# Zero products at the start of PE, GpSimd's scalar steps behind its edge fixes, transposes released by another x tile

## The chip, the cores and the metric

The kernel runs on one core of a Trainium2 chip. A core has a matrix engine (PE), a vector engine (VectorE, DVE in the profile), ScalarE (ACT), GpSimd (POOL) and a queue engine that issues transfers (SyncE, SP). The metric is device time in microseconds (us); lower is better. The kernel before takes 342.55 us, the median of six runs that lie between 342.0 and 345.52.

## The reference, cut to what matters

Input x has 2048 rows of 1024 values. Two branches are computed from it and mixed by a gate, row by row:

```python
g = sigmoid((x * gate_w).sum(-1, keepdims=True))
a = irfft2(rfft2(x) * (w_r + 1j * w_i))            # branch A, over both axes
Lam_bar = exp(dt * Lam)                            # branch B: a state space model, 1024 states
B_bar   = ((Lam_bar - 1) / Lam)[:, None] * Bmat
h_t = Lam_bar * h_(t-1) + B_bar @ x_t              # for each row t
y   = 2 * real(h @ Cmat.T) + x * Dskip
out = g * a + (1 - g) * y
```

## The kernel before, in words

Branch A is a two-dimensional FFT done as matrix products. Branch B does the products with B first, rotates the result by tables of cosines and sines so that the complex recurrence becomes a real one, runs it as a scan on VectorE, rotates back and multiplies by C. The two branches are woven together: a small planner (`merge`-like loops at L770 to L776 over two generators with hand-given costs) decides in which order their steps are written, and below it a scheduler of the language orders the instructions of PE, VectorE and ScalarE. SP and GpSimd run in the order in which the program is written (L189).

**The opening, which the change touches.** x is loaded in eight tiles of 512 KB, `xts[0]` to `xts[7]` (`load_x`, L201): the first four into the pool buffers "h", the last four into the space that later holds C (CT0). In between SP issues G_sb, M(0) and W(0). The ScalarE queue loads ident, four short vectors (vec8) and the Fourier matrix FW.

**The fold stage** (`fstage`, L464) takes one x tile at a time. VectorE writes the sums and differences of its halves into a tile `eo` (L468 to L471: even sum, even difference, and the same for the mirrored half). The mirrored half has one column that has no partner; GpSimd fixes these edges with four ops of two elements per partition (L473 to L476). L473 is needed for the products with the sums, L475 and L476 for those with the differences. After each odd tile, PE multiplies the two tiles with FW: four PSUM tiles (`ps_f`) of eight products of 256 columns each (L495, L496), 128 products in the whole stage; three PSUM buffers are in turn. ScalarE casts each PSUM tile out with two copies (L499, L500), 32 in all. The `eo` tiles rotate through two buffers "u" (even tiles) and two buffers "cu" (odd tiles); vec8 and `angk`, the scratch of the angle reduction, take their turns in "cu" as well.

**The scalar chain** (`scalars`, L305) is a generator that is stepped once per x tile. From the vectors it derives, on 128 x 8 values: dt and r (Exp on ScalarE, L307, L314), angles and their sines (L308 to L312; the sine needs a load of another function table on ScalarE), a complex quotient (L317 to L328), its magnitude by a Newton root (L329 to L335, ending in rho), its angle by a half-angle formula and Arctan (L337 to L350), and beta. GpSimd does a few of these steps: nrho = -rho (L336), beta's first half (L351), and the pair sg (L353, L354). rho and nrho scale the PSUM copies of branch B (L411), beta and thp make the tables (`tables`, L366).

**The transposes.** Behind tile 3 (L716 to L728) a VectorE copy of one element into BT[0] (L717) makes the DMA transposes of B and x wait for an x tile: SP issues `load_BT(0)`, `load_xT(0)`, M(1), W(1), BT(1), M(2), FI, M(3), BT(2), BT(3) behind it. xT(0), 512 columns of the transposed x, is the moving operand of branch B's first products (L409).

After the fold stage, the FFT (`fd` L507, `bf_w` L527, `w_mul` L547, `bi` L559, `idm` L578, `fi` L598) and branch B (`ssm_pe` L403, `ssm_dve` L415) run woven together until about 160 us, then the products with C (`half`, L821) and the mix, until the end.

The function that is touched contains nearly everything. A block for zero products stands at L249 to L253 already, with a loop over `range(0)`: its fill is issued on GpSimd, its products are not.

Of the kernel before, what the change touches and what calls it, by code (L numbers as in the profile page):

```python
# [12 lines left out]
FP32 = mybir.dt.float32  # L13
# [9 lines left out]
P = 128  # L23
TC = 512
# [112 lines left out]
def kernel(  # L137
# [17 lines left out]
    nc = tc.nc  # L155
# [18 lines left out]
    BT = cpool.tile([P, 8, 2, 8, P], BF16, name="BT")  # L174
    tab = cpool.tile([P, 8, 3, TC], BF16, name="tab")
# [4 lines left out]
    rp = ctx.enter_context(tc.tile_pool(name="rp", bufs=2))  # L180
    sm = ctx.enter_context(tc.tile_pool(name="sm", bufs=2))
    psU = ctx.enter_context(tc.tile_pool(name="psU", bufs=2, space=PSUM))
# [13 lines left out]
        nc.scalar.dma_start(out=vec8[:, i, :], in_=src.rearrange("(j p) -> j p", p=P))  # L196
    nc.scalar.dma_start(out=FW_sb, in_=cFW)

    x_v = x.rearrange("(p b) d -> p b d", b=16)

    def load_x(jj):  # L201
        if jj < 4:
            xt = hp.tile([P, 2, D], BF16, name="xt", tag="h")
        else:
            xt = CT0[:, 2 * (jj - 4):2 * (jj - 4) + 2].rearrange("p a b d -> p a (b d)")
        nc.sync.dma_start(out=xt, in_=x_v[:, 2 * jj:2 * jj + 2, :])
        return xt

    def load_BT(jb):
        for ri, src in enumerate((B_B_re, B_B_im)):  # L210
            nc.sync.dma_start_transpose(out=BT[:, jb, ri], in_=src[P * jb:P * (jb + 1), :])

    def load_xT(c, halves=(0, 1)):
        for h in halves:
            r0 = TC * c + 256 * h
            nc.sync.dma_start_transpose(out=xT[:, :, r0:r0 + 256], in_=x[r0:r0 + 256, :])
# [13 lines left out]
    def load_M(g):  # L230
        m = fr.tile([P, 6, P], BF16, name="MM", bufs=4)
        nc.sync.dma_start(out=m, in_=cMM[g])
        MM[g] = m

    def load_W(g):
        w = Wtiles[g % 2]
        for ri, src in enumerate((A_w_r, A_w_i)):
            rows = bass.AP(src.tensor, src.offset + g * 513, [[32 * 513, 64], [((32 - 2 * g) if g else 16) * 513, 2], [1, 513]])
            (nc.sync if g < 2 else nc.gpsimd).dma_start(out=w[:, ri, 0:513], in_=rows)
        WT[g] = w  # L240

    xts = [load_x(jj) for jj in range(5)]
# [3 lines left out]
    xts.append(load_x(6))  # L246
    load_W(0)
    xts.append(load_x(7))
    warm = BT[:, 6, 0, 0:4, :].rearrange("p a c -> p (a c)")  # L249
    nc.gpsimd.memset(warm, 0.0)  # L250
    wps = psU.tile([P, TC], FP32, name="wps", tag="psu")
    for _ in range(0):
        nc.tensor.matmul(wps, lhsT=warm[:, 0:P], rhs=warm, start=True, stop=True)  # L253
    vps = psU.tile([P, 4, 8], BF16, name="vps", tag="psu")
    for i in range(4):
        nc.tensor.transpose(out=vps[:, i, :], in_=vec8[:, i, :], identity=ident[0:8, 0:8])
# [6 lines left out]
    def v8(name):  # L263
        if name in ("r_sb", "thp", "beta", "rho", "nrho"):
            return sp.tile([P, 8], FP32, name=name)
        scr_n[0] += 1
        return scr[:, scr_n[0] - 1, :]
# [9 lines left out]
    nc.vector.memset(chpi, HALF_PI)  # L277
    r_sb, beta, rho, nrho = (v8(n) for n in ("r_sb", "beta", "rho", "nrho"))
    ang = sp.tile([P, 16], FP32, name="ang")
    angk = rp.tile([P, 2, 16], FP32, name="angk", tag="cu")  # L280
    snc = sp.tile([P, 2, 16], FP32, name="snc")
    thp = ang[:, 0:8]
    sTC, cTC = snc[:, 0, 8:16], snc[:, 1, 8:16]
# [3 lines left out]
    def frac(xx, kk, ff):  # L287
        nc.vector.tensor_scalar(out=kk, in0=xx, scalar1=MAGIC, scalar2=-MAGIC, op0=ALU.add, op1=ALU.add)
        nc.vector.tensor_sub(out=ff, in0=xx, in1=kk)
        nc.vector.tensor_scalar(out=kk.bitcast(I32), in0=ff.bitcast(I32), scalar1=0x7FFFFFFF, scalar2=None,  # L290
                                op0=ALU.bitwise_and)

    def v16():
        scr_n[0] += 2
        return scr[:, scr_n[0] - 2:scr_n[0], :]

    def rsqrt(y, x, s):
        nc.vector.tensor_scalar(out=y.bitcast(I32), in0=x.bitcast(I32), scalar1=-0.5, scalar2=float(0x5F3759DF),
                                op0=ALU.mult, op1=ALU.add)
        for _ in range(2):  # L300
            nc.vector.tensor_mul(out=s, in0=y, in1=y)
            nc.vector.scalar_tensor_tensor(out=s, in0=s, scalar=-0.5, in1=x, op0=ALU.mult, op1=ALU.mult)
            nc.vector.scalar_tensor_tensor(out=y, in0=s, scalar=1.5, in1=y, op0=ALU.add, op1=ALU.mult)

    def scalars():  # L305
        dt, are = v8("dt"), v8("are")
        nc.scalar.activation(out=dt, in_=ldt, func=ACT.Exp)  # L307
        nc.vector.scalar_tensor_tensor(out=thp, in0=lim, scalar=INV2PI, in1=dt, op0=ALU.mult, op1=ALU.mult)  # L308
        nc.vector.tensor_scalar_mul(out=ang[:, 8:16], in0=thp, scalar1=float(TC))
        frac(ang, angk[:, 0, :], angk[:, 1, :])  # L310
        nc.scalar.activation(out=snc[:, 0, :], in_=angk[:, 1, :], func=ACT.Sin, scale=TWO_PI_LO)
        nc.scalar.activation(out=snc[:, 1, :], in_=angk[:, 0, :], func=ACT.Sin, scale=-TWO_PI_LO, bias=chpi)  # L312
        nc.vector.tensor_mul(out=are, in0=dt, in1=lre)
        nc.scalar.activation(out=r_sb, in_=are, func=ACT.Exp)  # L314
        yield
        dd, inv = v16(), v8("inv")
        nc.gpsimd.tensor_mul(out=dd, in0=lam, in1=lam)  # L317
        nc.gpsimd.tensor_add(out=dd[:, 0, :], in0=dd[:, 0, :], in1=dd[:, 1, :])
        nc.vector.reciprocal(out=inv, in_=dd[:, 0, :])
        yield  # L320
        nl, pr, c2 = v16(), v16(), v16()
        nc.vector.tensor_mul(out=nl, in0=snc[:, ::-1, 0:8], in1=r_sb.unsqueeze(1).to_broadcast([P, 2, 8]))
        nc.vector.tensor_scalar_add(out=nl[:, 0, :], in0=nl[:, 0, :], scalar1=-1.0)
        nc.vector.tensor_mul(out=pr, in0=nl, in1=lam)
        nc.vector.tensor_add(out=c2[:, 0, :], in0=pr[:, 0, :], in1=pr[:, 1, :])
        nc.vector.tensor_mul(out=pr, in0=nl[:, ::-1, :], in1=lam)
        nc.vector.tensor_sub(out=c2[:, 1, :], in0=pr[:, 0, :], in1=pr[:, 1, :])
        yield  # L328
        m2, rs, mag, s = v8("m2"), v8("rs"), v8("mag"), v8("s")  # L329
        nc.vector.tensor_mul(out=pr, in0=c2, in1=c2)  # L330
        nc.vector.scalar_tensor_tensor(out=m2, in0=pr[:, 0, :], scalar=1e-30, in1=pr[:, 1, :], op0=ALU.add, op1=ALU.add)
        rsqrt(rs, m2, s)
        nc.vector.tensor_mul(out=mag, in0=m2, in1=rs)
        yield
        nc.vector.scalar_tensor_tensor(out=rho, in0=mag, scalar=2.0, in1=inv, op0=ALU.mult, op1=ALU.mult)  # L335
        nc.gpsimd.tensor_scalar_mul(out=nrho, in0=rho, scalar1=-1.0)  # L336
        hd = v8("hd")  # L337
        nc.vector.tensor_add(out=hd, in0=mag, in1=c2[:, 0, :])
        nc.vector.tensor_scalar_max(out=hd, in0=hd, scalar1=1e-20)
        nc.vector.tensor_mul(out=m2, in0=hd, in1=mag)  # L340
        yield
        rsqrt(rs, m2, s)
        nc.vector.tensor_mul(out=m2, in0=m2, in1=rs)
        nc.vector.scalar_tensor_tensor(out=hd, in0=m2, scalar=float(np.sqrt(2.0)), in1=hd, op0=ALU.mult, op1=ALU.add)
        nc.vector.reciprocal(out=hd, in_=hd)
        yield
        nc.vector.tensor_mul(out=hd, in0=c2[:, 1, :], in1=hd)
        nc.vector.tensor_scalar(out=hd, in0=hd, scalar1=-1.0, scalar2=1.0, op0=ALU.max, op1=ALU.min)
        fq = v8("fq")
        nc.scalar.activation(out=fq, in_=hd, func=ACT.Arctan)  # L350
        nc.gpsimd.tensor_scalar_mul(out=beta, in0=thp, scalar1=-255.5)  # L351
        nc.vector.scalar_tensor_tensor(out=beta, in0=fq, scalar=-2.0 * INV2PI, in1=beta, op0=ALU.mult, op1=ALU.add)
        nc.gpsimd.tensor_scalar_mul(out=sg[:, :, 1], in0=sTC, scalar1=-1.0)  # L353
        nc.gpsimd.tensor_copy(out=sg[:, :, 0], in_=sTC)  # L354
        yield

    chain = scalars()
    for _ in range(1):
        next(chain, None)
# [353 lines left out]
    for jj in range(8):  # L713
        for _ in fstage(jj):
            pass
        if jj == 3:  # L716
            nc.vector.tensor_copy(out=BT[0:1, 0, 0, 0, 0:1], in_=xts[4][0:1, 0, 0:1])  # L717
            load_BT(0)
            load_xT(0)
            load_M(1)  # L720
            load_W(1)
            load_BT(1)
            load_M(2)
            nc.sync.dma_start(out=FI_sb, in_=cFI)
            if 4 == 4:
                load_M(3)
            load_BT(2)
            load_BT(3)  # L728
# [165 lines left out]
```

## Time and profile before

| What | us |
|---|---|
| Median of six runs | 342.55 |
| The profiled execution, its own time | 342.56 |
| Its span on the core | 340.8 |
| PE busy (share of the span) | 322.8 (95%) |
| DVE busy | 286.7 (84%) |
| ACT busy | 189.9 (56%) |
| POOL busy | 52.7 (15%) |
| First x tile in use (L468) | 5.26 |
| Last cast of the fold stage starts (L500) | 29.02 |
| First step on W in branch A (L551) | 35.08 |

Times in the profile count from the start of the span. A row of the timeline gives start, duration, engine, line, operation, output and inputs, how many were merged, and in brackets how long the engine had been idle and what ended it. Durations of neighbouring instructions overlap[...]: how fast a series runs is read from the distance between starts. A row of the waits gives who waited for whom, the total, the number of waits and the longest. PEclk is the clock that the throttle granted.

### The profile page before, as it was taken

Reading aid. Unit: us, or ns where it says so; the run is one execution under the profiler, and the core shown is the slowest. Engines: PE = TensorE matmul, PEld = TensorE weight load, DVE = VectorE, ACT = ScalarE, POOL = GpSimd, SP = SyncE. Lnnn points to the kernel's source line nnn. Section 1 sums busy time; section 2 is a strip of 40 time slices with the busy share of each in tenths; the row PEclk is TensorE's granted clock in tenths of the full one; section 3 lists DMA queues with packets and bytes.
Section 4 is the critical chain, followed back from the end, with each engine's and each line's share of the span. In section 5 each row is a group of like instructions: output and inputs, shape, how many; then the busy total and the mean of one; then the engine's idle time right before and its main releaser. Section 6 shows DMA issues by size and latency. Waiting matters only on the chain.

```text
span 340.8 us, 4928 instructions
## 1 busy us (share of the span) xinstructions
PE 322.8 (95%) x1804; PEld 172.8 (51%) x1804; DVE 286.7 (84%) x418; ACT 189.9 (56%) x266; POOL 52.7 (15%) x101
## 2 busy tenths in 40 slices
PE   2879999999999999998999999999999999999995
PEld 1666666665656566553444444444444444444442
DVE  2874899999999997999997999599999999982311
ACT  2789799889898777696253424441424424443200
POOL 4450322221211000000011002010120121201100
PEclk9999999999999999999999999999999999999999
DMA  6999999799879113022897063942855664969721
GB/s 241 388 219 196 170 234 219 143 241 165 197 176 180 63 62 125 31 92 94 250 220 211 0 185 67 266 90 71 188 111 135 156 170 108 242 191 245 201 65 46
DMA packets 70712, 54.97 MB, mean 161 GB/s; under 512 B 52768, under 2 KB 57888, under 8 KB 70688
## 3 DMA queue, kind: packets, MB, share of 16 engines
q1 hardware_dynamic: 64144, 38.75, 44.6%
q0 software_dynamic: 6192, 15.74, 21.7%
q8 instruction: 14, 0.23, 0.3%
q10 hardware_dynamic: 352, 0.17, 0.2%
q14 instruction: 10, 0.08, 0.1%
HBM read 21.61 MB, written 8.39 MB: 88 GB/s over the span
## 4 chain that ended last, share of the span: by engine, by line
PE 68%; DVE 12%; ACT 3%; DMA 3%; issue 2%; DVEq 0%; ACTq 0%; SPq 0%
PE psy L830 32%; PE psu L409 25%; PE ps_id L583 3%; DVE su L429 2%; DVE t L552 2%; DMA CT<-in_B_C_re_dram 2%; DVE Y L551 1%; DMA ya_scratch<-ya 1%; DVE Y L553 1%; PE ps_y L602 1%; DVE Y L554 1%; PE ps_d L512 1%; PE ps_y L605 1%; PE ps_y L603 1%; PE ps_y L604 1%
## 5 line engine op out<-in xcount | busy, mean ns | idle before, releaser
L409 PE MATMUL psu<-xT,BT 128*128 128x512 bf16 x512 | 120.0, 379 | 1.0 <-ACT u L411 1.0
L409 PEld LDWEIGHTS <-BT 128*128 128x128 bf16 x512 | 49.4, 98 | 56.2 <-issue 1.7
L429 DVE TENSOR_TENSOR_SCAN su<-r_sb,carry,cu 128x512 bf16<-128x512 f32 x48 | 57.8, 1265 | 0.4
L411 ACT ACTIVATE u<-psu,rho 128x512 bf16<-128x512 f32 x32 | 22.2, 694 | 51.7 <-PE psu L409 49.2
L411 ACT ACTIVATE u<-psu,nrho 128x512 bf16<-128x512 f32 x32 | 22.2, 693 | 37.6 <-PE psu L409 37.6
L830 PEld LDWEIGHTS <-h 128*128 128x128 bf16 x256 | 25.0, 98 | 30.2
L815 POOL DMA_DIRECT2D xf<-gac x16 | 16.3, 1019 | 117.6 <-DMA big<-in_B_C_im_dram 67.7
L837 DVE SCALAR_TENSOR_TENSOR o<-psy,om_f,xf 128x1024 bf16<-128x1024 f32 (+1 forms) x17 | 20.6, 1216 | 15.2 <-PE psy L830 15.2
L830 PE MATMUL psy<-CT,h 128*128 128x512 bf16 x128 | 28.9, 379 | 0.0
L830 PE MATMUL psy<-big,h 128*128 128x512 bf16 x128 | 28.9, 379 | 0.0
L812 ACT ACTIVATE gac<-gac,gf 128x1024 bf16<-128x1024 bf16 x16 | 18.2, 1139 | 18.5 <-DMA gac<-ya_scratch 18.5
L808 DVE TENSOR_TENSOR xc<-xc,dsk_bc 128x1024 bf16<-128x1024 bf16 x16 | 10.9, 684 | 15.4 <-DMA xc<-in_A_x_dram 14.9
L420 DVE TENSOR_TENSOR cu<-u,tab 128x2048 bf16<-128x2048 bf16 x16 | 19.5, 1218 | 1.9 <-ACT u L411 1.7
L830 PEld LDWEIGHTS <-xT 128*128 128x128 bf16 x128 | 12.5, 98 | 15.1
L830 PEld LDWEIGHTS <-big 128*128 128x128 bf16 x128 | 12.5, 98 | 15.1
L424 DVE TENSOR_TENSOR cu<-cu,su 128x2048 bf16<-128x2048 bf16 x16 | 19.6, 1228 | 0.4
L422 DVE TENSOR_TENSOR su<-u,tab 128x2048 bf16<-128x2048 bf16 x16 | 19.5, 1217 | 0.0
L512 PE MATMUL ps_d<-G_sb,big 128*128 128x256 bf16 (+3 forms) x128 | 18.6, 286 | 0.3 <-ACT X L539 0.3
L429 DVE TENSOR_TENSOR_SCAN su<-r_sb,cu 128x512 bf16<-128x512 f32 x16 | 18.7, 1208 | 0.1
L814 ACT ACTIVATE xf<-xc,om_f 128x1024 f32<-128x1024 bf16 x16 | 18.2, 1138 | 0.2
L496 PE MATMUL ps_f<-BT,eo 128*128 128x256 bf16 x64 | 16.5, 301 | 1.9 <-POOL eo L473 1.9
L495 PE MATMUL ps_f<-BT,eo 128*128 128x256 bf16 x64 | 16.5, 302 | 1.5 <-DVE eo L468 1.5
(163 smaller groups left out, 562.3 us busy)
## 6 DMA issues: line engine op xcount, KB each, us to landing
xf<-gac POOLq DMA_DIRECT2D x16, 512.0 KB, 6.8
ya_scratch<-ya SPq DMA_DIRECT2D x16, 256.0 KB, 2.0
xc<-in_A_x_dram SPq DMA_DIRECT2D x16, 256.0 KB, 4.4
gac<-ya_scratch SPq DMA_DIRECT2D x16, 256.0 KB, 3.7
out_dram<-o SPq DMA_DIRECT2D x15, 256.0 KB, 2.3
MM<-c_MM SPq DMA_DIRECT2D x16, 192.0 KB, 3.8
xt<-in_A_x_dram SPq DMA_DIRECT2D x4, 512.0 KB, 4.8
CT<-in_A_x_dram SPq DMA_DIRECT2D x4, 512.0 KB, 8.0
```

The source lines that it names most:

```text
L409: nc.tensor.matmul(psu, lhsT=BT[:, jb, ri, dblk, :], rhs=xT[:, dblk, TC * c:TC * (c + 1)], start=(dblk == 0), stop=(dblk == 7))
L411: nc.scalar.activation(out=u[:, jj, ri, :], in_=psu, func=ACT.Copy, scale=(nrho if ri else rho)[:, jb:jb + 1])
L420: nc.vector.tensor_mul(out=cu, in0=u, in1=tq[:, :, 0:1, :].to_broadcast(full))
L422: nc.vector.tensor_mul(out=su, in0=u[:, :, ::-1, :], in1=tq[:, :, 1:3, :])
L424: nc.vector.tensor_add(out=cu, in0=cu, in1=su)
L429: nc.vector.tensor_tensor_scan(out=su[:, jj, ri, :], data0=r_sb[:, jb:jb + 1].to_broadcast([P, TC]), data1=cu[:, jj, ri, :], initial=(0.0 ...
L495: nc.tensor.matmul(ps[:, jl], lhsT=lo, rhs=FW_sb[:, 0:2 * P], start=(i == 0), stop=False)
L512: nc.tensor.matmul(ps[:, lo:lo + w], lhsT=FX[:, q, 8 * g:8 * g + 8, :], rhs=G_sb[:, o:o + w], start=start, stop=stop, skip_group_check=True)
L812: nc.scalar.activation(out=gac, in_=gac, func=ACT.Copy, scale=gf[:, tb:tb + 1])
L814: nc.scalar.activation(out=xf, in_=xc, func=ACT.Copy, scale=om_f[:, tb:tb + 1])
L830: nc.tensor.matmul(psy[:, ds], lhsT=hs[c, jb // 2][:, jb % 2, ri, P * tq:P * (tq + 1)], rhs=CT[dh][:, jb, ri, :], start=(i == 0), stop=(i ...
L837: nc.vector.scalar_tensor_tensor(out=o[:, ds], in0=psy[:, ds], scalar=om_f[:, tb:tb + 1], in1=xfs[tb][:, ds], op0=ALU.mult, op1=ALU.add)
```

## The change

Four edits, all in the opening:

- The zero block moves to the front of PE's work, its fill goes to VectorE, and twelve products of 128 x 512 zeros into a PSUM tile that nobody reads are issued ahead of the vec transposes.
- `angk` moves from a pool buffer "cu" into a corner of the table space `tab`, which is written much later.
- nrho, beta's first half and sg are issued one step of the scalar chain later, in one group behind the edge fixes of tile 6, where nrho stood ahead of those of tile 4 and the others ahead of those of tile 6.
- The one-element copy that releases the transposes reads `xts[3]` instead of `xts[4]`.

```diff
+    warm = BT[:, 6, 0, 0:4, :].rearrange("p a c -> p (a c)")
+    nc.vector.memset(warm, 0.0)
+    wps = psU.tile([P, TC], FP32, name="wps", tag="psu")
+    for _ in range(12):
+        nc.tensor.matmul(wps, lhsT=warm[:, 0:P], rhs=warm, start=True, stop=True)
+
     x_v = x.rearrange("(p b) d -> p b d", b=16)
...
-    warm = BT[:, 6, 0, 0:4, :].rearrange("p a c -> p (a c)")
-    nc.gpsimd.memset(warm, 0.0)
-    wps = psU.tile([P, TC], FP32, name="wps", tag="psu")
-    for _ in range(0):
-        nc.tensor.matmul(wps, lhsT=warm[:, 0:P], rhs=warm, start=True, stop=True)
     vps = psU.tile([P, 4, 8], BF16, name="vps", tag="psu")
...
-    angk = rp.tile([P, 2, 16], FP32, name="angk", tag="cu")
+    angk = tab[:, 7, 2, 0:64].bitcast(FP32).rearrange("p (a n) -> p a n", a=2)
...
-        nc.gpsimd.tensor_scalar_mul(out=nrho, in0=rho, scalar1=-1.0)
         hd = v8("hd")
...
         nc.scalar.activation(out=fq, in_=hd, func=ACT.Arctan)
+        yield
+        nc.gpsimd.tensor_scalar_mul(out=nrho, in0=rho, scalar1=-1.0)
         nc.gpsimd.tensor_scalar_mul(out=beta, in0=thp, scalar1=-255.5)
...
         if jj == 3:
-            nc.vector.tensor_copy(out=BT[0:1, 0, 0, 0, 0:1], in_=xts[4][0:1, 0, 0:1])
+            nc.vector.tensor_copy(out=BT[0:1, 0, 0, 0, 0:1], in_=xts[3][0:1, 0, 0:1])
             load_BT(0)
```

## The prediction

> **What bounds it now.** I read the busy time in stretches first, to see which engine is full where, then the waits of the first 40 us, then the timeline of the first 37 us engine by engine. The chain of work that ended last is of no use here: it can be followed back only to 37.18 us, and the change lies before that. Columns of the first fence: stretch, its length, busy us of PE, PEld, DVE, ACT, POOL, then the clock shown, DMA share and GB/s.
>
> ```profile
> 5.00:10.00 5.00, 2.05 (x10) 1.11 (x11) 3.32 (x15) 1.73 (x4) 2.04 (x8) 1.00 0.97 340
> 10.00:15.00 5.00, 5.00 (x28) 3.65 (x29) 3.90 (x18) 3.37 (x8) 3.66 (x10) 1.00 1.01 397
> 20.00:25.00 5.00, 4.38 (x39) 3.70 (x40) 3.40 (x18) 3.39 (x9) 4.21 (x19) 1.00 1.22 227
> 25.00:30.00 5.00, 5.00 (x42) 3.59 (x40) 3.71 (x9) 5.00 (x11) 0.03 (x1) 1.00 0.76 161
> 80.00:120.00 40.00, 38.57 (x258) 24.27 (x256) 39.24 (x62) 34.61 (x49) 6.36 (x9) 1.00 0.74 150
> ```
>
> From 40 to 120 us VectorE is full (39.24 of 40), after 160 us the chain is back-to-back PE work. Neither has slack, so an earlier start of that stage passes through to the end. In the opening nothing is full throughout; ScalarE becomes full from 21.77 to 37 us. Its 32 PSUM casts (L499/L500) pace the fold stage:
>
> ```profile
> 8.14 1.28 ACT L311 ACT_TABLE_LOAD   x1
> ...
> 10.39 0.31 ACT L312 ACTIVATE snc<-angk,chpi 128x16 f32<-128x16 f32 x1 [0.20 <-DVE angk L290]
> 11.84 0.58 ACT L499 CAST big<-ps_f 128x512 bf16<-128x512 f32 x1 [1.14 <-PE ps_f L496]
> ...
> 19.46 0.70 ACT L500 CAST big<-ps_f 128x512 bf16<-128x512 f32 x1
> 21.77 0.58 ACT L499 CAST big<-ps_f 128x512 bf16<-128x512 f32 x1 [1.61 <-PE ps_f L496]
> 22.25 0.59 ACT L500 CAST big<-ps_f 128x512 bf16<-128x512 f32 x1
> ...
> 24.63 0.27 ACT L350 ACTIVATE scr<-scr 128x8 f32<-128x8 f32 x1
> 24.74 0.64 ACT L499 CAST big<-ps_f 128x512 bf16<-128x512 f32 x1
> ...
> 29.02 0.77 ACT L500 CAST big<-ps_f 128x512 bf16<-128x512 f32 x1
> ```
>
> The casts follow each other every 0.477 us (start to start; the durations overlap). The last starts at 29.02. The mark for this prediction is that start: all ScalarE work up to 37.3 us hangs on it without a gap. Lost in front of it: 1.61 us at 21.77, and a first cast only at 11.84. Why, the PE and POOL rows and the waits say:
>
> ```profile
> 13.94 0.42 PE L495 MATMUL ps_f<-BT,eo 128*128 128x256 bf16 x1
> 14.15 0.32 PE L496 MATMUL ps_f<-BT,eo 128*128 128x256 bf16 x1
> 14.30 0.27 PE L495 MATMUL ps_f<-BT,eo 128*128 128x256 bf16 x1
> 14.41 0.27 PE L496 MATMUL ps_f<-BT,eo 128*128 128x256 bf16 x1
> ```
> ```profile
> POOL nrho L336 <- DVE scr L338: 4.8, 1, 4.8
> PE ps_f L496 <- POOL eo L473: 1.9, 2, 1.4
> DVE eo L468 <- PE ps_f L496: 1.1, 1, 1.1
> ```
>
> Products start every 0.2145 us from 9.91 until 14.15, then every 0.109: PE runs at half rate until 4.24 us into its first unbroken stretch, although the clock column says 1.00 throughout; the cadence is what to read. And GpSimd stands at nrho (L336) until VectorE has rho (19.16), with the edge fix of x tile 4 (L473, run at 19.65) queued behind it; PE, then ScalarE, wait for that edge.
>
> **The change, part by part.** Spacings I use, all from the timeline: fold op to the next instruction 0.34; small op to an independent fold op 0.08 to 0.10; dependent small op to the next 0.20; product 0.109 (half rate 0.2145); cast 0.477. The built program's order of the new kernel gives the sequence on each engine.
>
> *Zero products.* The zero fill moves from GpSimd (0.52 at 0.84) to VectorE, which waits for x until 5.26: free. Twelve 128x512 products start near 1.2 us. The row for that shape at full rate is L409's 0.216 spacing (8 in 1.73); at half rate twice that, 0.43. Twelve take at most 5.2 us, to 6.4. Queued behind them are the four vec transposes, which wait for their loads until 6.58 anyway: cost 0 (if the cover were gone, one for one). What they buy: by this trace's 4.24 us the rate doubles near 5.5, before x arrives. The Trainium skill ("TensorE: Matmul & The Clock Gate", Part 1) says the gate opens after a busy window of about 3.4 us that runs freely, so about 4.6 to 5.6; it says also, against this change, that an idle window of that length closes it, and (Part 4) that transposes do not count as busy in the same way. Between 6.4 and 8.5 PE has only the four transposes and half a dozen products. The nearest row is kind: PE idles 1.37 us before 20.10 and comes back at 0.109. By the row the rate holds, by the strict reading it can fall. I take the row, and keep the other as a case.
>
> *angk leaves the "cu" buffers.* Not in the title, but the program order shows that it matters. Today x tile 1's sums take the buffer of the vec loads, so VectorE does tile 2 before it finishes tile 1: tile 1's L470 runs only at 10.27. Now tile 1 has a fresh buffer. It landed by 7.41 (SP's M load, which reuses its completion semaphore, issues then). So VectorE: L272 at 7.28, tile 1's L468 at 7.40, L470 at 8.07 to 8.49. PE has ten products from there to the end of the first tile needed: 10 x 0.109 + 0.2, so the first cast is at 9.8 instead of 11.84.
>
> *What is late next: ScalarE's order.* Two of those two microseconds are not kept. The table load (1.28 us), hidden in an idle stretch today, now stands behind cast 2: casts 1 and 2 with L314 between them from 9.8 to 10.95, table load to 12.25, L311 and L312 to 12.73, cast 3 at 12.65, where it was 12.79. And VectorE's L322 waits for L312: 12.75 instead of 11.74 (it has finished tile 3 and the release copy by 12.2, so it idles 0.5).
>
> *nrho, beta and sg behind the edge fixes.* Four GpSimd ops of 0.2 to 0.44 move, none is added. L473 of tile 4 no longer waits for rho: it can run once the tile has landed (11.6) and PE has freed its buffer (about 12). The PE stalls of 1.37 and 0.52 and ScalarE's 1.61 go. Queued behind the moved ops now are tile 7's edges and the wait for beta: four ops after tile 6's edges (about 20) end near 21.2, and tile 7's first fold op is at 21.2, Arctan at 22.2, so nothing waits. First user of nrho is the copy at 34.79: hidden.
>
> *What is late after that: the Arctan.* In the new order it stands behind cast 21 (today behind 22) and waits for VectorE's L348. From L322 to L348 there are 14 fold spacings x 0.34 (4.76), 10 x 0.08 (0.80), 16 x 0.20 (3.20), and five short ones (0.48): 9.24 us. L348 starts at 21.99, ends 22.2. ScalarE would reach cast 22 at 12.65 + 19 x 0.477 = 21.7, so it stands about half a microsecond. Arctan 22.25, cast 22 at 22.36, cast 32 at 22.36 + 10 x 0.477 = **27.13, 1.89 us before 29.02**. Without the Arctan wait it would be 26.6, 2.4 earlier; that is the upper bound.
>
> *Transposes released by the fourth tile.* In the built program the first transpose still waits for the completion semaphore that the fifth tile's load used (11.6; the profile of before has SPq L211 waiting 0.9 us for just that), and the copy now stands behind tile 3's four fold ops: 12.2. So SP is released 0.36 us later, not earlier, with every load behind it. The DMA engines are full with x, G, M and W until 17 us (350 to 418 GB/s), so between 0 and 0.4 us of that reaches the transposes; I take 0.4. xT's second half was issued at 20.02 and took 6.5 us: landed at 26.5, now up to 26.9. PE asks for it about 26.6. PE can stand until 27.1 before ScalarE's L524 is late. So it is hidden, by 0.2 us.
>
> Sum: the profiled execution has span 340.8 and time 342.56, 1.76 us around the span; the median of six runs is 342.55, the same. 342.56 - 1.89 = **340.7 us**.
>
> **Rivals.**
> *The clock falls back, or never rises.* Ten products at 0.2145 make the first cast 1.05 later, and it passes through table load, L322 and Arctan. Gain 0.84: 341.7. For: two thin microseconds; against: the row at 20.10.
> *The gain is given back later.* A transfer or another VectorE order in 40 to 160 us absorbs it: 342.5. For: the new order differs in a few places beyond 28 us (two L409 products earlier, L386 and L576 swapped). Against: VectorE is full there and the transfers are issued by the same stages, so they move too.
> *More than I think.* VectorE's small ops hide better between folds, the Arctan wait is gone: 340.1.
> *Slower: the transposes.* If later release lets all four first transposes issue as slowly as the second did (3.80 us each, 15.2 instead of 11.0 for the four), xT lands near 31.1. Each microsecond past 27.1 costs one, and past 29.0 the kernel is slower than before: 2.1 us, 344.7. For: the release is later in program order; against: the slow issues belong to the full DMA stretch that ends at 17.
> Were the third edit to do what it says, nothing would change: xT is not waited for.
>
> **Numbers.** Likeliest, 340.7 (own range 340.1 to 341.3): 0.60. More: 0.07. Clock: 0.15. Given back: 0.12. Slower: 0.06. About 0.5%, 1.71 us, can be told from no change, so faster is below 340.84: three quarters or more of the likeliest case and the "more" case, 0.54. Same 0.40, slower 0.06. Range 339.9 to 342.2: it leaves out the slow case, most of "given back" near 342.5, and a little below.
>
> **What would show it.** Right: product spacing 0.109 from tile 1 on; first cast near 9.8; table load between casts 2 and 3; no PE wait for L473; Arctan preceded by a short ScalarE wait on VectorE; last cast near 27.1; first transposes issued no earlier than 11.8. Wrong: products at 0.21 after 8.5; a ScalarE or PE wait for xT between 26 and 32; or a last cast at 27 with a first Y (L551, 35.08) not 1.9 earlier, or a span that does not follow it.

## The result, and the profile after

| | before | changed |
|---|---|---|
| Median, us (runs) | 342.31 (73) | 340.43 (36) |
| Ratio of the times, 95% interval | | 0.9941 (0.9926 to 0.9956) |
| The profiled execution, us | 342.56 | 339.83 |
| Its span, us | 340.8 | 337.8 |
| Last cast of the fold stage starts | 29.02 | 26.57 |
| First step on W (Y, L551, now L553) | 35.08 | 32.58 |
| First pm (VectorE's sums in branch A's last stage, L676, now L678) | 111.06 | 109.27 |

By the interval the gain is 1.5 to 2.5 us. Ratios, here and below, are of fast runs alone (a few runs, over 1.5% above the fastest, are left out), so they are not quite the quotient of the medians. In the changed file the lines lie one to two further on (L499 is L501, L551 is L553, L717 is L719), and in the moved zero block more.

The stretches of the changed kernel, columns as before:

```profile
5.00:10.00 5.00, 4.54 (x29) 2.61 (x28) 4.26 (x18) 1.25 (x4) 3.65 (x12) 1.00 0.99 336
20.00:25.00 5.00, 4.37 (x37) 3.26 (x36) 4.76 (x17) 4.41 (x11) 1.68 (x7) 1.00 1.26 192
80.00:120.00 40.00, 38.57 (x256) 24.25 (x255) 39.25 (x61) 34.62 (x48) 5.16 (x7) 1.00 0.67 147
```

PE's 2.05 us between 5 and 10 have become 4.54, of which about 1.5 are zero products; between 20 and 25 ScalarE's 3.39 have become 4.41. The stretch from 80 to 120 us is what it was (39.24 and 39.25 on VectorE), so nothing was won or lost there. ScalarE's timeline shows the casts:

```profile
8.96 0.58 ACT L501 CAST big<-ps_f 128x512 bf16<-128x512 f32 x1 [1.44 <-PE ps_f L498]
...
10.15 1.28 ACT L312 ACT_TABLE_LOAD   x1
...
11.76 0.56 ACT L501 CAST big<-ps_f 128x512 bf16<-128x512 f32 x1
...
21.70 0.21 ACT L350 ACTIVATE scr<-scr 128x8 f32<-128x8 f32 x1 [0.59 <-DVE scr L348]
21.82 0.57 ACT L502 CAST big<-ps_f 128x512 bf16<-128x512 f32 x1
...
26.57 0.70 ACT L502 CAST big<-ps_f 128x512 bf16<-128x512 f32 x1
```

The order is the one foretold: two casts, the table load behind them, an unbroken row of casts, one wait of 0.59 for VectorE at the Arctan, and the row again to the end. In this pair of executions the last cast comes 2.45 us earlier. Products on PE, and the GpSimd instructions that had stood in each other's way:

```profile
1.17 5.30 PE L203 MATMUL wps<-BT 128*128 128x512 bf16 x12 [1.17 <-DVE chpi L278]
...
7.28 0.27 PE L498 MATMUL ps_f<-BT,eo 128*128 128x256 bf16 x1
7.39 0.27 PE L497 MATMUL ps_f<-BT,eo 128*128 128x256 bf16 x1
...
8.42 0.28 PE L498 MATMUL ps_f<-BT,eo 128*128 128x256 bf16 x1 [0.41 <-DVE eo L472]
```
```profile
12.21 0.20 POOL L475 TENSOR_TENSOR eo<-CT 128x2 bf16<-128x2 bf16 x1
...
19.74 0.23 POOL L352 TENSOR_SCALAR nrho<-rho 128x8 f32<-128x8 f32 x1
```

The first separate products are 0.109 apart, so PE is at full rate from the first x tile on. The edge of tile 4 is fixed at 12.21 instead of 19.65, nrho follows at 19.74.

Not all of the 2.45 arrives. VectorE's timeline and ScalarE's, near 40 and 155 us:

```profile
39.06 0.69 DVE L553 TENSOR_TENSOR Y<-X,W 128x1028 bf16<-128x1028 bf16 x1 [0.44 <-ACT X L541]
40.48 0.69 DVE L554 TENSOR_TENSOR t<-X,W 128x1028 bf16<-128x1028 bf16 x1 [0.73 <-DMA W<-in_A_w_i_dram]
```
```profile
154.78 0.59 ACT L609 CAST ya<-ps_y 128x512 bf16<-128x512 f32 x1 [1.14 <-DMA ya_scratch<-ya]
```

The third step on W now waits 0.44 for ScalarE's copy of X and then 0.73 for its own W tile, neither of which it waited for before, and the first pm is only 1.79 earlier. The row of ScalarE had this form before:

```profile
158.65 0.59 ACT L607 CAST ya<-ps_y 128x512 bf16<-128x512 f32 x1 [3.22 <-DMA ya_scratch<-ya]
```

In this one execution of before, ScalarE waited 3.22 us for a store, and the span from the first pm to the end is 229.7 us instead of 228.5. That is why the two profiled spans differ by 3.0, though the opening accounts for 1.79 only: 2.45 - 0.66 given back near 40 us + 1.2 at the store = 3.0. The wait for the store goes with the zero products: it is 1.13 or 1.14 us in all nine profiled executions that have them, and 1.5 to 3.2 in the five that don't (the column "store" below). How the two hang together no run here shows, and so it is not shown either how much of the median's 1.88 us comes from the opening and how much from the store.

### The profile page after: what moved, and what is told of

Same layout as the page of the kernel before. It is cut to its first block, busy times and chain, and to the rows that moved or that the text cites. A ratio compares the mean times of both kernels' runs of the same rounds, so it can differ in the third digit from the quotient of the medians.

```text
span 337.8 us, 4956 instructions
## 1 busy us (share of the span) xinstructions
PE 326.1 (97%) x1816; PEld 173.0 (51%) x1816; DVE 287.5 (85%) x419; ACT 189.8 (56%) x266; POOL 52.0 (15%) x100
## 4 chain that ended last, share of the span: by engine, by line
PE 70%; DVE 16%; ACT 6%; DMA 5%; issue 2%; POOL 0%; DVEq 0%; ACTq 0%; POOLq 0%
PE psy L832 33%; PE psu L411 27%; PE ps_id L585 3%; DMA xt<-in_A_x_dram 3%; DVE t L554 2%; DVE su L431 2%; DMA W<-in_A_w_i_dram 2%; DVE Y L553 1%; DVE Y L555 1%; PE ps_y L604 1%; PE ps_y L607 1%; PE ps_y L606 1%; PE ps_y L605 1%; DVE Y L556 1%; ACT big L502 1%
## 5 line engine op out<-in xcount | busy, mean ns | idle before, releaser
L814 ACT ACTIVATE gac<-gac,gf 128x1024 bf16<-128x1024 bf16 x16 | 18.2, 1139 | 16.3 <-DMA gac<-ya_scratch 16.3
L816 ACT ACTIVATE xf<-xc,om_f 128x1024 f32<-128x1024 bf16 x16 | 18.2, 1139 | 0.2
L578 ACT CAST big<-ps_q 128x1024 bf16<-128x1024 f32 x16 | 16.3, 1020 | 2.9 <-PE ps_q L577 2.5
L526 ACT CAST X<-ps_d 128x1024 bf16<-128x1024 f32 x16 | 16.3, 1034 | 2.2 <-PE ps_d L514 1.8
```

Of the source, the lines that this page charges most:

```text
L526: nc.scalar.copy(out=X1, in_=ps)
L814: nc.scalar.activation(out=gac, in_=gac, func=ACT.Copy, scale=gf[:, tb:tb + 1])
L816: nc.scalar.activation(out=xf, in_=xc, func=ACT.Copy, scale=om_f[:, tb:tb + 1])
```

## The experiments

Before had medians of 342.27 (35 runs), 342.54 (19) and 342.54 (29) in the three groups (e1 to e4, e5 to e8, e9 to e12), and every ratio is to before. The first table has the times, the second where they come from, read from each kernel's profiled execution.

| | Kernel | Median (runs) | Ratio, 95% interval |
|---|---|---|---|
| e1 | before + zero products | 341.18 (12) | 0.9975 (0.9950 to 1.0000) |
| e2 | before + angk moved | 340.79 (12) | 0.9969 (0.9937 to 1.0001) |
| e3 | before + GpSimd steps moved | 341.49 (12) | 0.9986 (0.9958 to 1.0014) |
| e4 | changed, no zero products | 341.42 (12) | 0.9973 (0.9947 to 1.0000) |
| e5 | changed, again | 340.13 (7) | 0.9912 (0.9881 to 0.9944) |
| e6 | changed, angk back | 340.18 (8) | 0.9929 (0.9900 to 0.9959) |
| e7 | changed, GpSimd steps back | 339.97 (9) | 0.9935 (0.9903 to 0.9968) |
| e8 | changed + W(2) early | 339.66 (8) | 0.9909 (0.9879 to 0.9939) |
| e9 | changed, release back | 340.44 (12) | 0.9943 (0.9924 to 0.9962) |
| e10 | e4 once more | 341.05 (12) | 0.9958 (0.9932 to 0.9984) |
| e11 | changed, release later | 340.58 (12) | 0.9962 (0.9938 to 0.9987) |
| e12 | changed + early release + W(2) early | 339.43 (6) | 0.9921 (0.9891 to 0.9951) |

By their intervals none of e1, e2 and e3 is clear of no change, and the intervals of e4 to e12 all overlap that of the changed kernel: the times alone rank none of them.

The vectors' loads land at slightly different times in each execution. The column "from first use" counts from the row that first uses them (L270 of before at 7.18, L271 of the changed kernel at 7.09). Each row is one execution. The two of the changed kernel differ by 0.23 in this column, and an x tile that lands late adds up to a microsecond (e9), so a smaller difference between two rows proves little by itself. "Store" is ScalarE's wait for `ya_scratch` near 155 us.

| | Last cast | from first use | PE waits for xT | L554 waits for W(2) | first pm - last cast | store | span - first pm |
|---|---|---|---|---|---|---|---|
| before | 29.02 | 21.84 | - | - | 82.04 | 3.22 | 229.7 |
| changed | 26.57 | 19.48 | - | 0.73 | 82.70 | 1.14 | 228.5 |
| e1 | 28.05 | 21.34 | - | - | 82.01 | 1.14 | 228.5 |
| e2 | 26.38 | 19.92 | - | 0.61 | 82.71 | 2.83 | 229.3 |
| e3 | 27.74 | 21.14 | - | - | 82.26 | 1.56 + 0.25 | 228.5 |
| e4 | 25.95 | 19.51 | 1.86 | - | 83.91 | 3.03 | 229.5 |
| e5 | 26.47 | 19.25 | 1.03 | - | 83.23 | 1.14 | 228.5 |
| e6 | 26.68 | 19.52 | 0.44 | 1.02 | 83.24 | 1.14 | 228.6 |
| e7 | 27.93 | 21.08 | - | - | 82.01 | 1.13 | 228.6 |
| e8 | 27.02 | 19.60 | - | - | 82.27 | 1.13 | 228.5 |
| e9 | 27.64 | 20.77 | - | - | 82.25 | 1.13 | 228.5 |
| e10 | 27.04 | 19.52 | 0.84 | - | 82.89 | 1.50 + 0.31 | 228.6 |
| e11 | 26.96 | 19.71 | - | 0.71 | 82.69 | 1.14 | 228.6 |
| e12 | 27.73 | 20.80 | - | - | 82.25 | 1.14 | 228.5 |

Without a wait for xT or W(2), the first pm comes 82.01 to 82.04 us after the last cast where GpSimd's steps stand as before (before, e1, e7), and 82.25 to 82.27 where they are moved (e3, e8, e9, e12): there the third step on W waits 0.44 to 0.46 for ScalarE's copy of X. So the moved steps give back a quarter of a microsecond. A wait for xT or W(2) adds most of its length to that: 0.73 gives 82.70, 0.84 gives 82.89, 1.86 gives 83.91. And the span ends 228.5 us after the first pm, or up to 1.2 later with the longest waits at the store (before, e2, e4).

**e1, the zero products alone.** The edit puts the zero block of the changed kernel into before:

```diff
+    nc.vector.memset(warm, 0.0)
...
+    for _ in range(12):
+        nc.tensor.matmul(wps, lhsT=warm[:, 0:P], rhs=warm, start=True, stop=True)
```


> The kernel before with the zero products alone (twelve, fill on VectorE). Theory (the time follows the start of the fold stage's last cast, and the zero products pay because PE takes tile 1 at full rate): products 0.109 apart from the start; first cast near 10.3 instead of 11.84; the wait of PE for L473 of tile 4 stays, because nrho still stands ahead of it, so cast 17 comes with rho, near 20.9; last cast near 28.1, time about 0.9 us under before (341.4 where before is 342.3). Rival (the clock is the whole gain): last cast near 26.6 and 2.0 us under before. Rival (GpSimd's order is the whole gain): last cast at 29.0, no change.

Measured: 341.18. The first cast is at 11.39, which from the first use is where it was (4.68, before 4.66), and the two stalls in the middle stay: PE waits 1.7 us for L474 and ScalarE 1.41 at cast 17. From the first use, the last cast comes 0.5 earlier. But this execution is no test of full rate: PE's products are 0.2145 apart again from 10.56 to 13.93, and here the clock column (before the DMA share) shows it:

```profile
11.00:13.00 2.00, 2.00 (x11) 1.40 (x10) 1.95 (x11) 1.61 (x4) 1.84 (x6) 0.50 0.99 358
```

What the zero products alone would bring to the fold stage at the full clock is therefore not shown.

**e2, angk alone.**

```diff
-    angk = rp.tile([P, 2, 16], FP32, name="angk", tag="cu")
+    angk = tab[:, 7, 2, 0:64].bitcast(FP32).rearrange("p (a n) -> p a n", a=2)
```


> The kernel before with angk in the table space alone. In its program order tile 1 is done in one go, the table load stands behind cast 2, PE is at half rate, nrho still stands ahead of the edges. Theory: first cast near 9.6 to 10.9, but cast 3 and VectorE's L322 not before 13, rho about a microsecond later than 19.0, and the edges of tile 4 wait for it: last cast at 29 to 30, time 0 to 1 us over before. Rival (angk's place is the hidden key of the change): last cast at 28 or earlier, 1 us under before.

Measured: 340.79, and in the marks nearly the whole change: first cast at 8.65, last cast at 26.38, 19.92 from the first use. I had expected far less of it. GpSimd's timeline has the reason:

```profile
16.59 0.46 POOL L336 TENSOR_SCALAR nrho<-rho 128x8 f32<-128x8 f32 x1 [4.72 <-DVE scr L338]
17.01 0.20 POOL L473 TENSOR_TENSOR eo<-CT 128x2 bf16<-128x2 bf16 x1
```

nrho still stands ahead of tile 4's edge, but it ran at 16.59 where it had waited until VectorE had rho at 19.16. In the new order of VectorE, rho comes 4.8 us after L322 instead of 7.3; of these 2.5 us, 1.1 are VectorE's wait for PE's products in before (`DVE eo L468 <- PE ps_f L496`), which is gone. The edge is fixed at 17.01, and what was a PE stall of 1.37 and 0.52 is 0.54 and 0.25. So angk's place weakens the GpSimd stall too, which the prediction ascribed to another edit.

**e3, the GpSimd steps alone.**

```diff
-        nc.gpsimd.tensor_scalar_mul(out=nrho, in0=rho, scalar1=-1.0)
...
+        yield
+        nc.gpsimd.tensor_scalar_mul(out=nrho, in0=rho, scalar1=-1.0)
```


> The kernel before with GpSimd's scalar steps behind the edge fixes alone. Theory: PE's 1.9 us and ScalarE's 1.6 us of waiting for L473 go, cast 17 at 19.9 instead of 21.8; then the Arctan, behind cast 22, waits for VectorE's L348, which has not moved (23.4 to 23.6): cast 23 at 23.8, last cast at 28.1, 0.9 us under before. Rival (the stall is worth its full length): last cast at 27.4, 1.6 us under. Rival (clock alone): no change.

Measured: 341.49. The PE waits for nrho's queue are gone; the last cast comes 0.7 earlier from the first use. The first cast is as late as ever (11.10). ScalarE stands 0.29 and 0.63 for PE at 13.45 and 15.15.

**e4 and e10, the changed kernel without zero products.**

```diff
-    for _ in range(12):
+    for _ in range(0):
```


> The changed kernel without the zero products, all else as changed. Theory: PE at half rate until about 12.7; first cast 0.5 late (9.5), cast 3 near 12.3, VectorE's L322 and the Arctan late by the same half microsecond: last cast near 27.1 instead of 26.57, time 0.5 us over the changed kernel, 1.4 under before. Rival (the clock is the whole gain): last cast near 29, time as before. Rival (the zero products are only ballast): the changed kernel's time.

> The changed kernel without its zero products, once more. Theory (they bring nothing that the opening can keep; where this kernel lost before, xT had landed late by chance): last cast again 19.3 to 19.8 past the first use of the vectors, time that of the changed kernel, 340.0 to 340.6. Rival (the half rate costs something of its own, by the products' order or by when PE frees buffers): 341.2 to 341.6 again, with a PE wait for xT of more than 1 us.

Measured: 341.42 and 341.05. PE ran its fold products 0.2145 apart until 11.38 in e4 and 12.03 in e10. The first cast came 2.19 after the first use in both, against 1.87 in the changed kernel: 0.3 later. Then it is gone. VectorE's L323 stands 5.12 after the first use in both (changed 5.09), and the last cast 19.51 and 19.52 (changed 19.48). So with the other edits in, the zero products bring nothing in the fold stage. The medians are higher than the changed kernel's all the same, by 0.6 to 1.3 us (though the intervals overlap), and my expectation of e10's time fell. Both traces have the PE wait for xT; in e4 it is this:

```profile
27.44 0.38 PE L411 MATMUL psu<-xT,BT 128*128 128x512 bf16 x1 [1.86 <-DMA xT<-in_A_x_dram]
```

xT landed about 27.3 and 27.4 in these two, 25.8 to 26.9 in the executions with zero products, and 26.4 to 26.5 in before, e2 and e3, which have none either. So a late xT does not follow from leaving them out. The longer wait at the store (3.03, and 1.50 + 0.31) does go with it in every execution; how, no run here shows.

**e5, the changed kernel again.**

> The changed kernel itself once more, as the yardstick beside the next three on one chip: ratio to before 0.994, last cast 19.5 us after the first use of the vectors (L271, that is L270 of before). The landing of the first loads moved by half a microsecond between executions so far, so the marks of the opening are read from L271 on. Theory (the wait for W(2) at 40 us, 0.73, and the shorter wait for the ya store at 154, 1.1 instead of 3.2, are chance of one execution): they differ here. Rival (both belong to the change): they return.

Measured: 340.13. The wait at the store is 1.14 again. The wait for W(2) is not there, but one for xT has taken its place:

```profile
27.10 0.59 PE L411 MATMUL psu<-xT,BT 128*128 128x512 bf16 x2 [1.03 <-DMA xT<-in_A_x_dram]
```

**e6, angk put back in the changed kernel** (e2's edit undone).

> The changed kernel with angk back in the cu buffer. In its program order tile 1 still comes before tile 2 on VectorE, mixed with the angle steps, and the table load stands ahead of the first cast. Theory (what counts is that tile 1 comes first, which the zero products bring about as well as angk's place does): last cast 19.6 to 20.4 after L271 (changed kernel 19.5), time within 0.5 us of the changed kernel. Rival (angk's place is the gain, since alone it gave as much as everything together): last cast 21 or more after L271, about 1.5 us over the changed kernel.

Measured: 340.18, no slower than the changed kernel, and the last cast is 19.52 from the first use. ScalarE's timeline:

```profile
9.00 1.28 ACT L312 ACT_TABLE_LOAD   x1
...
11.47 0.59 ACT L501 CAST big<-ps_f 128x512 bf16<-128x512 f32 x1 [0.72 <-PE ps_f L498]
```

The first cast is 2.5 us later, as in before, but the table load lies in front of it, L322 is not held up, and no wait at the Arctan is left. The early first cast of the changed kernel is spent on just these two.

**e7, the GpSimd steps put back** (e3's edit undone).

> The changed kernel with nrho, beta and sg on GpSimd where they were. Theory: tile 4's edge waits for rho again, now at 17.2; cast 17 comes near 19.3 instead of 18.4, but the Arctan's wait of 0.59 takes most of it up: last cast 0.3 to 0.9 later (19.8 to 20.4 after L271), time 0.3 to 0.9 over the changed kernel. Rival (this edit is worth the full stall of before): 1.6 over. Rival (it is worth nothing once tile 1 comes first): the changed kernel's time.

Measured: 339.97. Here the stall is back: PE waits 1.21 and 0.86 for L474, ScalarE 1.58. The last cast is 21.08 from the first use, 1.6 later than in the changed kernel; but in this execution VectorE also waited 1.22 us for the fourth x tile (changed: 0.19). If that wait passes through in full, about 0.6 of the 1.6 is the edit's. The time shows none of it: with a last cast at 27.93 neither the xT nor the W(2) wait occurs, and the first pm is 0.2 to 0.7 after the changed kernel's two.

**e8, W(2) loaded early.** It takes away the wait at the third step on W by giving W(2) its own space, free until the tables are made there:

```diff
+    W2 = tab[:, 6, 0:3, :].rearrange("p a n -> p (a n)")[:, 0:1028].rearrange("p (a n) -> p a n", a=2)
...
-        w = Wtiles[g % 2]
+        w = W2 if g == 2 else Wtiles[g % 2]
...
-        if g + 2 < 16:
+        if 0 < g < 14:
             load_W(g + 2)
...
+    load_W(2)
```


> The changed kernel with W(2) loaded into unused table space right behind the fold stage, rather than when W(0) has been used. Theory (two thirds of a microsecond of the shift is given back at 40 us, where VectorE waits for W(2)): the wait of 0.73 before the third t (L554) is gone, the shift of 2.4 us at the third Y lasts to the first pm at 109, time 0.5 us under the changed kernel. Rival (VectorE's order or ScalarE's X copies hold that place anyway): the wait is replaced, time as the changed kernel.

Measured: 339.66. The wait is gone, the one for ScalarE's copy of X (0.44) stays, and the first pm is 82.27 after the last cast instead of 82.70. So W(2) held 0.43 of the 0.66 us given back. Against the changed kernel in the same group (340.13) the intervals overlap, and no gain in time is shown.

**e9, the release put back** to the fifth x tile, in the changed kernel:

```diff
-            nc.vector.tensor_copy(out=BT[0:1, 0, 0, 0, 0:1], in_=xts[3][0:1, 0, 0:1])
+            nc.vector.tensor_copy(out=BT[0:1, 0, 0, 0, 0:1], in_=xts[4][0:1, 0, 0:1])
```


> The changed kernel with one edit undone: the copy that releases the transposes reads xts[4] again. Theory (this edit does nothing, because the copy stands behind tile 3's fold ops either way and the fifth tile has landed by then): first transpose at 12.1 to 12.6, time that of the changed kernel, 340.1 to 340.5. Rival (the fifth tile lands later than the copy's turn, so the edit earned its wait): the copy waits for a DMA, first transpose at 12.8 or later, PE waits for xT, 340.8 to 341.3.

Measured: 340.44. The copy waits for nothing. It runs at 12.78, later than 12.12, and the first transpose issues at 12.94, because the fold ops ahead of the copy were late:

```profile
11.28 0.42 DVE L470 TENSOR_TENSOR eo<-xt 128x512 bf16<-128x512 bf16 x1 [1.07 <-DMA xt<-in_A_x_dram]
```

That is the fourth x tile's landing (the copy stands behind these ops, and nothing that the edit touches stands ahead). It makes most of the 1.3 us by which the last cast is later from the first use.

**e11, the release later.** The copy goes to GpSimd, behind the edges of tile 4:

```diff
-        if jj == 3:
-            nc.vector.tensor_copy(out=BT[0:1, 0, 0, 0, 0:1], in_=xts[3][0:1, 0, 0:1])
+        if jj == 4:
+            nc.gpsimd.tensor_copy(out=BT[0:1, 0, 0, 0, 0:1], in_=xts[4][0:1, 0, 0:1])
```


> The changed kernel with the release later: the one-element copy runs on GpSimd behind the edge fixes of tile 4 (about 14.5, where the copy on VectorE ran at 12.1). Theory (xT's landing is what the fold stage now runs into): xT lands 1.2 to 2.4 later, at 27.8 to 29, PE waits 1.5 to 2.5 for it, first Y 1 to 2 later, 341.3 to 342.4. Rival (the transposes issue faster once the full DMA stretch is over, so that the delay is made up, or PE's slack takes it): no wait over 0.8, 340.2 to 340.8.

Measured: 340.58, and my theory fell. SP's timeline in the changed kernel and in e11:

```profile
12.28 2.37 SPq L217 DMA_TRANSPOSE BT<-in_B_B_re_dram  x1
14.70 3.48 SPq L217 DMA_TRANSPOSE BT<-in_B_B_im_dram  x1
18.23 4.86 SPq L222 DMA_TRANSPOSE xT<-in_A_x_dram  x2
```
```profile
14.89 1.33 SPq L217 DMA_TRANSPOSE BT<-in_B_B_re_dram  x1
16.27 2.09 SPq L217 DMA_TRANSPOSE BT<-in_B_B_im_dram  x1
18.40 5.08 SPq L222 DMA_TRANSPOSE xT<-in_A_x_dram  x2
```

The first transpose issues 2.61 us later, the third only 0.17: the two ahead of it take less time to issue. PE does not wait for xT. The release is not what sets xT's landing, within these 2.6 us.

**e12, release and W(2) both early.** e8's edit, the copy one tile earlier on `xts[2]`, and `load_W(0)` behind `load_xT(0)`:

```diff
-    load_W(0)
...
-        if jj == 3:
-            nc.vector.tensor_copy(out=BT[0:1, 0, 0, 0, 0:1], in_=xts[3][0:1, 0, 0:1])
+        if jj == 2:
+            nc.vector.tensor_copy(out=BT[0:1, 0, 0, 0, 0:1], in_=xts[2][0:1, 0, 0:1])
             load_BT(0)
             load_xT(0)
+            load_W(0)
```


> The changed kernel with xT and W(2) both taken off the path: the copy stands one tile earlier and reads xts[2], W(0) is issued behind xT(0) instead of ahead of x tile 7, and W(2) is loaded into the table space before the woven stage. Theory (xT's landing and the W(2) load are the two places that eat the gain): first transpose at 10.5 to 11.6, no PE wait for xT, no wait of L554 for W, 339.2 to 339.8. Rival (earlier transposes share the full DMA stretch and only push the last x tiles back): tile 7 lands 0.5 or more later, last cast as much later, 340.2 to 341.

Measured: 339.43, the lowest median, from six runs; its interval overlaps those of the changed kernel and of e8, so it is not shown to beat either. The profiled execution was the slowest of the six. In it the first transpose issued at 10.39, took 5.20 us to issue, and the third began at 18.90, no earlier than in e11. VectorE waited 1.63 us for the fourth x tile, the longest such wait seen, as the rival had it. PE's clock also fell in it, as in e1: its products are 0.2145 apart from 14.8 to 18.2 (the clock column reads 0.50 from 15 to 17), and ScalarE waited 0.62 for PE at 18.43. So its late last cast is not the early release's alone. Neither the xT nor the W(2) wait occurs.

## Why the prediction was right, and where its sum was not

The likeliest case stood at 340.7, with 1.89 us gained; the median is 340.43, and the interval of the gain is 1.5 to 2.5. In the opening the mechanism is as foretold, in both executions of the changed kernel. But the 1.89 came out near the measured gain partly by luck: the opening gained 0.56 more than I worked out, 0.66 was given back that I had at nothing, and the store, which I had not looked at, may have a part in the median. One of my own signs of being wrong did appear: in e5 PE waited 1.03 us for xT.

- **Zero products: cost 0.** Right in the changed kernel's profile. Twelve took 5.30 us, all at half rate, to 6.47, later than the 5.5 at which I had the rate double; the vec transposes began at 6.41. It is not certain everywhere: without zero products the second transpose began at 5.8 to 6.9, and in e1 all four ran back to back from 6.41, so there they may have been held up. The rate was full from the first x tile. That four transposes and thin work let it fall again did not happen here; in e1 and e12 the clock did fall, but only after 10.5 and 14.8. And the price set on losing it, 1.05 us passing through, was wrong: e4 and e10 ran at half rate to 11.4 and 12.0 and lost 0.3 at the first cast and nothing at the last. VectorE's fold ops and the release copy keep L323 back in any case; in e4 and e10 the sine came just behind them (in e10 it ends at 12.61, and L323 starts at 12.64).
- **First cast at 9.8.** It came at 8.96. The term that was mis-sized is "ten products from there": VectorE's op that PE waited for (L472) ended at 8.37, about as worked out (8.49), but only the products at 8.42, 8.54 and 8.65 were left for the first PSUM tile, three and not ten: 8.42 + 3 x 0.109 + 0.2 = 8.95.
- **Table load behind cast 2.** Right, at 10.15 (said: about 10.95), by the same 0.8. Cast 3 at 11.76 instead of 12.65.
- **L322 at 12.75.** 12.18 (it is L323 now). It no longer waited for the sine (done by 11.85), but for VectorE's own fold ops of tile 3. So of the 0.84 won at the first cast 0.57 stayed.
- **9.24 us from there to L348, then Arctan.** 9.33; L348 at 21.51, Arctan at 21.70 after a wait of 0.59 (said: about half a microsecond). Right. VectorE's two rows:

```profile
12.18 0.15 DVE L323 TENSOR_TENSOR scr<-snc,r_sb 128x16 f32<-128x16 f32 x1
...
21.51 0.16 DVE L348 TENSOR_SCALAR scr<-scr 128x8 f32<-128x8 f32 x1
```

- **Last cast at 27.13.** 26.57: 0.56 earlier, all of it from the 0.57 at L322. From the first use of the vectors it is 2.36 earlier than in before.
- **GpSimd.** The order is right and tile 4's edge waits for nothing. I said that nothing would wait for the tile 7 edges behind the moved steps; PE did, 0.63 at 22.14 for L477. But that edge had itself waited 0.50 for VectorE, not for the moved steps, which were done by 20.74; and the casts behind the Arctan ran on without a gap, so it cost nothing. What the moved steps did cost came later: the quarter of a microsecond at the third step on W.
- **The edits as separate gains.** This is where the reasons fell short. I gave the end of the 1.61 us stall to the GpSimd move alone. e2 nearly ends it with angk alone, since rho comes 2.5 us sooner after L322; e6 shows that with the other edits in, angk brings nothing, and e7 that without the GpSimd move only about 0.6 us of the fold stage is lost (if the late x tile passes through in full), and no time that can be measured. In the last cast from the first use, e1, e2 and e3 gain 0.5, 1.9 and 0.7, which would sum to 3.1, and all together give 2.36: e2 and e3 shorten the same stall. The times can't show this. By the ratios the three gains sum to 2.4 us, each with an interval that reaches about zero, and all together give 2.0.
- **Everything passes through.** Not quite. Of 2.45 us 1.79 reach the first pm. ScalarE's copy of X takes a quarter of a microsecond, and the wait that takes the rest is W(2) at 40 us in one execution of the changed kernel and xT at 26 to 27 in the other (e5). I put "given back later" at 0.12 and as all or nothing; it is partial and stands in the likeliest case. All six executions with a last cast before 27.0 have one of the two waits; of the eight with a later one only e10 (27.04) has, though e8 (27.02) and e12 load W(2) early. So about there the loads begin to bound the opening, and I had named xT alone as near.
- **Transposes.** "Not earlier, and hidden": 12.28 against 11.84, and xT was ready at 26.02 in the profiled run. That the third edit does nothing is shown by e9. "Hidden by 0.2 us" was too sure: xT came later than PE asked in e4, e5, e6 and e10. The slower rival, transposes that issue slowly after a late release, is answered by e11, where the later release issued faster. My reason against it was wrong all the same: slow issues do not simply belong to the full DMA stretch, for e11's first transpose issued in 1.33 us between 14 and 16, when the DMA engines were full (share 1.05, 404 GB/s).

What stays open: why the wait at the store is longer in every execution without zero products, how much of the median gain comes from there, and whether the 0.6 to 1.3 us by which the medians of e4 and e10 lag are that or the luck of xT's landing.

## What to carry to other kernels

Two edits that each shorten a stall may shorten the same one: try each alone and each left out, and count by marks (last cast, first pm), for the parts need not add. When an opening is made shorter, look for the loads that were just hidden, and give each its landing time and the moment it will be asked for; here xT and W(2) took 0.4 to 1.6 us back in turn. A difference between two profiled executions is split by stage before it is believed: here 1.2 of 3.0 us lay in a store wait 120 us behind the edits. And look at the clock of each stage before a trace is read: in two of fourteen the mean over the whole run hid 3.4 us at half clock inside the stage in question.

## What was unexpected of the hardware

- The issue of the same DMA transpose took 1.33, 2.37 or 5.20 us on SP, for a release at 14.9, 12.3 and 10.4; the third transpose began at 18.2 to 18.9 in these three. So an earlier release only made the issue longer.
- Without zero products PE's product spacing went from 0.2145 to 0.109 us 3.2 us (e2, 6.44 to 9.69), 4.5 (e10) and 5.0 (e4) after its first products, and in e3 5.9 after the start of an unbroken stretch (9.18 to 15.10), while the clock column read 1.00 in all of them. The same twelve zero products took 5.30 us, all at half rate, in the changed kernel's profile, and 4.89, 4.43 and 4.35 in e7, e12 and e9, where the rate doubled inside the block. The later falls in e1 and e12, for 3.4 us each, the column did show, as 0.50.
- The wait of VectorE for the fourth x tile was 0.19 us in the changed kernel and 1.07, 1.22 and 1.63 in e9, e7 and e12. In e9 and e7 the loads ahead of it are the same as in the changed kernel: the landing of one 512 KB tile varies by as much as an edit is worth here.
- ScalarE's wait for the store near 155 us was 1.13 or 1.14 us in nine of nine executions with zero products, which end before 7 us, and 1.5 us or more in five of five without.
